# Attention with sink and window heads, then a gated feed-forward block: the order of all instructions from a list schedule in place of fixed interleaving

## Chip, cores, metric

One core of one Trainium2 chip. The metric is the device time of a run in microseconds (us), lower is better.

## What is computed

Four sequences of 768 positions, eight heads of 64. Heads 0, 2 and 6 attend to all earlier positions; the other five only to the first 4 positions and to the last 64. The attention output, 3072 x 512, goes through a gated block with weights 512 x 1536, 512 x 1536 and 1536 x 512.

```python
scores = scale * np.matmul(q, k.transpose(0, 1, 3, 2))
stream_keep = causal & (is_sink | in_win)
mask = np.where(retr[0, :, 0, 0, None, None], full_mask, stream_mask)
...
a = np.exp(scores)
a = a / (np.sum(a, axis=-1, keepdims=True) + 1e-09)
attn_out = np.matmul(a, v)
...
x = np.ascontiguousarray(attn_out.transpose(0, 2, 1, 3)).reshape(B * S, H * D)
g = x @ w_gate
silu = g * (1.0 / (1.0 + np.exp(-g)))
return silu * (x @ w_val) @ w_out
```

## The kernel before

Work is cut into 24 tiles of 128 positions; a pair is two tiles of one sequence (`QP`, 12 pairs, in the order sequence 0, 1, 0, 0, 1, 1, then 2 and 3). Tiles are gathered into seven groups of 2, 2, 4, 4, 4, 4, 4 (`SIZES`), over which the feed-forward block runs, so its matmuls have 256 columns in groups 0 and 1 and 512 in the others.

Of a pair: `load` brings queries, keys and values (512 KB each) into one of 11 `raw` buffers on the sync queue; `cast` makes half precision copies (`hq`; ScalarE for queries and keys, for pairs 0 and 1 VectorE and GpSimd for keys; GpSimd for values); `transposes` turns queries and keys by TensorE, eight 128 x 128 transposes at a time, into the one buffer `tr`, and VectorE evacuates them into `qkT` (L231). Calls go by row parity j, so that scores need both calls of a pair. GpSimd then copies the keys and values of sinks and of the previous block (`k2`, `v2`).

Of a tile: units of up to eight score matmuls into the one buffer `sc` (L292), the exponential by ScalarE into one of seven buffers `e` (L298, L302), masks multiplied in (`masks`; GpSimd, the large ones of the first four tiles VectorE), value matmuls for odd and for even heads into the one buffer `av` (L340), normalisation by VectorE (L343, L344), four transposes (`xtr`, L357) and their copy into the group's `xt` (L358).

Of a group: twelve times a gate quad (four matmuls, L446), tanh by ScalarE (L450), a val quad (L457) and two VectorE steps (L461, L464) that leave `h`. Gates and vals share three buffers of accumulator memory. Then per tile three quads of output matmuls (L480), one copy by ScalarE (L493) and a store on the sync queue. Weights are cast by ScalarE and GpSimd in turn (`wcast`), 12 gate and val pieces of 256 columns within group 0, six output pieces within group 1.

The order is written out. `items` is one list of attention steps, woven unit by unit (`weave`). In the loop over groups, after each gate, val or output quad a `beat` runs the masks left over and a fixed share of that list: group g's beats are spread evenly over the attention of group g + 1. Each engine takes its instructions in the order in which the program issues them, with waits on semaphores; `tc.manual_schedule()` leaves that order as it is.

Of the kernel before, what the change touches and what calls it, by code (L numbers as in the profile page):

```python
# [11 lines left out]
PSUM = bass.MemoryType.PSUM  # L12


@with_exitstack
def kernel(
# [13 lines left out]
    nc = tc.nc  # L30
# [15 lines left out]
    QP += [(b, n) for b in range(2, B) for n in range(NT // 2)]  # L46
    TILES = [(b, 2 * n + m) for b, n in QP for m in range(2)]
# [11 lines left out]

    ctx.enter_context(tc.manual_schedule())  # L60

    const = ctx.enter_context(tc.tile_pool(name="const", bufs=1))
    raw = ctx.enter_context(tc.tile_pool(name="raw", bufs=11))
    half = ctx.enter_context(tc.tile_pool(name="half", bufs=2))
    epool = ctx.enter_context(tc.tile_pool(name="epool", bufs=7))
    xpool = ctx.enter_context(tc.tile_pool(name="xpool", bufs=3))
    small = ctx.enter_context(tc.tile_pool(name="small", bufs=4))
    xtp = ctx.enter_context(tc.tile_pool(name="xtp", bufs=2))
    ffns = ctx.enter_context(tc.tile_pool(name="ffns", bufs=2))
    hpool = ctx.enter_context(tc.tile_pool(name="hpool", bufs=2 * NJ))  # L70
    opool = ctx.enter_context(tc.tile_pool(name="opool", bufs=2))
    ps_gv = ctx.enter_context(tc.tile_pool(name="ps_gv", bufs=3, space=PSUM))
    ps_o = ctx.enter_context(tc.tile_pool(name="ps_o", bufs=1, space=PSUM))
    ps_sc = ctx.enter_context(tc.tile_pool(name="ps_sc", bufs=1, space=PSUM))
    ps_av = ctx.enter_context(tc.tile_pool(name="ps_av", bufs=1, space=PSUM))
    ps_tr = ctx.enter_context(tc.tile_pool(name="ps_tr", bufs=1, space=PSUM))

# [8 lines left out]
    wod = moe_w_out.rearrange("(po p) n -> p po n", p=128)  # L86
    landed = {}

    def load(what):
        r = raw.tile([128, 1024], FP, name="raw", tag="raw")  # L90
        landed[what] = r
        kind, n = what
# [22 lines left out]
    def wcast(eng, kind, n):  # L115
# [6 lines left out]
        if eng is nc.scalar:  # L122
            eng.copy(out=dst, in_=src)
        else:
            eng.tensor_copy(out=dst, in_=src)
        freed()

    def whole(n):
        return [(kd, n) for kd in "qkx"]

    order = whole(0) + whole(1) + [(kd, n) for n in range(6) for kd in "gv"]
    order += whole(2) + whole(3) + [("o", n) for n in range(6)]
    order += [x for n in range(4, len(QP)) for x in whole(n)]
    at = [0]

    def freed(n=1):

        for _ in range(n):
            if at[0] < len(order):
                load(order[at[0]])  # L140
                at[0] += 1

    freed(11)


    ident = const.tile([128, 128], FH, name="ident")
    nc.gpsimd.memset(ident, 0.0)
    nc.gpsimd.affine_select(
        out=ident, in_=ident, compare_op=ALU.not_equal, fill=1.0,
        base=0, pattern=[[-1, 128]], channel_multiplier=1,  # L150
    )

    def keep(ap, base, qstep, kstep):
        nc.gpsimd.affine_select(
            out=ap, in_=ap, compare_op=ALU.is_ge, fill=0.0, base=base,
            pattern=[[qstep, 128]], channel_multiplier=kstep,
        )

    m0 = const.tile([128, 8, 128], FH, name="m0")
    m1 = const.tile([128, 2, 128], FH, name="m1")
    diag = const.tile([128, 128], FH, name="diag")
    band0 = const.tile([128, 128], FH, name="band0")
    nc.gpsimd.memset(diag, 1.0)
    keep(diag, 0, 1, -1)
    nc.gpsimd.memset(band0, 1.0)
    keep(band0, WIN - 1, -1, 1)
    nc.gpsimd.memset(band0[0:NSINK, :], 1.0)  # L170
    keep(band0, 0, 1, -1)
    nc.gpsimd.memset(m1, 1.0)
    keep(m1[:, 0, :], WIN - 1, -1, 1)
    keep(m1[:, 0, :], 0, 1, -1)
    keep(m1[:, 1, :], WIN - 1 - 128, -1, 1)
    nc.gpsimd.memset(m1[0:64, 1, :], 0.0)
    nc.gpsimd.memset(m1[0:NSINK, 1, :], 1.0)


    qkT = [const.tile([128, 2, 4, S], FH, name=f"qkT{n}") for n in range(2)]  # L180
    k2 = [const.tile([128, 4, 4, 128], FH, name=f"k2_{n}") for n in range(2)]
    vt = [const.tile([128, NT, 8, 66], FH, name=f"vt{n}") for n in range(2)]
    v2 = [const.tile([128, 4, 8, 66], FH, name=f"v2_{n}") for n in range(2)]
    for n in range(2):
        nc.gpsimd.memset(vt[n][:, :, :, 64:66], 1.0)
        nc.vector.memset(k2[n][:, :, :, 0:64], 0.0)
        nc.vector.memset(v2[n][0:64], 0.0)
    for n_, src in enumerate((band0, band0, band0, diag, band0, band0, diag, diag)):
        nc.vector.tensor_copy(out=m0[:, n_, :], in_=src)


    warm = ps_gv.tile([128, 512], FP, name="warm", tag="gv")
    for n in range(40):
        nc.tensor.matmul(warm[:, 0:128], ident, ident, start=True, stop=True)


    halves = {}

    def cast(n):

        b, pi = QP[n]
        hq = half.tile([128, 2, 2, 2, 256], FH, name="hq", tag="hq")
        for w, kd in enumerate("qk"):
            r = landed.pop((kd, n)).rearrange("p (h j d) -> p h j d", j=2, d=64)
            for j in range(2):
                o_ = hq[:, w, j].rearrange("p r (k d) -> p r k d", d=64)
                i_ = r[:, :, j].rearrange("p (k r) d -> p r k d", r=2)
                if n < 2 and w == 1:
                    (nc.gpsimd if j else nc.vector).tensor_copy(out=o_, in_=i_)
                else:  # L210
                    nc.scalar.copy(out=o_, in_=i_)  # L211
            freed()
        r = landed.pop(("x", n)).rearrange("p (m h d) -> p m h d", m=2, d=64)
        for m in range(2):
            nc.gpsimd.tensor_copy(out=vt[b % 2][:, 2 * pi + m, :, 0:64], in_=r[:, m])
        freed()
        halves[n] = hq

    def transposes(n, j):
        b, pi = QP[n]  # L220
        hq = halves[n]
        if n == 0 and j:
            tr = ps_gv.tile([128, 2, 4, 128], FH, name="tr", tag="gv")
        else:
            tr = ps_tr.tile([128, 2, 4, 128], FH, name="tr", tag="tr")
        for w in range(2):
            for p in range(4):
                nc.tensor.transpose(  # L228
                    tr[:, w, p, :], hq[:, w, j, p // 2, (p % 2) * 128:(p % 2 + 1) * 128], ident)
        T = qkT[b % 2]  # L230
        nc.vector.tensor_copy(  # L231
            out=T.rearrange("p w r (n j) -> p w r n j", j=2)[
                :, :, :, pi * 128:(pi + 1) * 128, j],
            in_=tr)
        if j == 0 or pi == 0:
            return
        K2, V, V2 = k2[b % 2], vt[b % 2], v2[b % 2]
        if pi == 1:
# [7 lines left out]
        for m in (2 * pi - 1, 2 * pi):
            nc.gpsimd.tensor_copy(
                out=K2[:, :, m - 1, 64:128], in_=T[:, 1, :, m * 128 + 64:(m + 1) * 128])
            nc.gpsimd.tensor_copy(out=V2[64:128, m - 1], in_=V[64:128, m])
# [19 lines left out]
    av_blocks = {}  # L269
    deferred = []  # L270

# [9 lines left out]

    def scores(t, u, unit):
        b, i = TILES[t]
        T = qkT[b % 2]
        sc = ps_sc.tile([128, 2, 4, 128], FP, name="sc", tag="sc")
        e = epool.tile([128, 2, 4, 128], FH, name="e", tag="e")
        for n in range(4):
            for s in range(2):
                if n < len(unit[s]):
                    h, _, _, kk, vv = unit[s][n]  # L290
                    p = SIDE[h][0]
                    nc.tensor.matmul(  # L292
                        sc[:, s, n, :], kk,
                        T[s * 64:s * 64 + 64, 0, p, i * 128:(i + 1) * 128])
                    av_blocks.setdefault((t, h), []).append((e[:, s, n, :], vv))
# [271 lines left out]
```

## Time and profile before

| | us |
|---|---|
| median of 3 runs (lowest, highest) | 300.4 (299.0, 302.36) |
| the profiled execution's own time | 300.72 |
| its span, first to last instruction | 299.0 |
| mean granted TensorE clock, share of full speed | 0.952 |
| busy: TensorE, VectorE, ScalarE, GpSimd | 264.3, 174.6, 147.8, 132.2 |

The span is what the profile's times refer to, from its first instruction; the execution's own time holds 1.7 us around it. PE is TensorE, PEld its weight loads, DVE VectorE, ACT ScalarE, POOL GpSimd, SP the sync engine, whose queue issues all loads and most stores. Matmuls are pipelined, so the busy time of one overlaps that of the next.

### The profile page before, as it was taken

The page shows a single profiled execution, that of the slowest core. Times are in us where ns is not written, and L with a number is a line of the kernel's source. Part 1 is how long each engine was busy: PE and PEld are TensorE (multiplying, and loading weights), DVE is VectorE, ACT ScalarE, POOL GpSimd, SP SyncE. Part 2 cuts the span into 40 slices and gives each one's busy share as a digit, 9 for nine tenths or more (in the row PEclk, how much of TensorE's full clock was granted, in tenths as well). Part 3 has the DMA queues.
Part 4 walks back from the last instruction along what each step waited for, and adds up shares of the span by engine and source line. Part 5 has one row for each costly group of instructions (what it writes and reads, how often), then busy time and mean ns, then how long its engine had stood idle before and what let it go on. Part 6 is the DMA issues. An engine that isn't in the chain of part 4 may idle for free.

```text
span 299.0 us, 5710 instructions
## 1 busy us (share of the span) xinstructions
PE 264.3 (88%) x2232; PEld 144.2 (48%) x2232; DVE 174.6 (58%) x331; ACT 147.8 (49%) x242; POOL 132.2 (44%) x195
## 2 busy tenths in 40 slices
PE   7356687869898997989999999999999998999995
PEld 7244465646564454544454545544454444444442
DVE  5546665844648476676675566784676455555500
ACT  3443838784493753825546653726444552232221
POOL 6172568893884641485536333476424230000000
PEclk9758879986999999999999999999999999999998
DMA  7999999999134170441310001001100001001012
GB/s 206 327 382 381 267 355 353 255 289 283 39 95 153 30 217 1 115 134 37 70 37 35 4 33 37 35 2 37 37 36 2 35 35 37 0 35 37 35 70 105
DMA packets 61514, 34.96 MB, mean 117 GB/s; under 512 B 26032, under 2 KB 57008, under 8 KB 61488
## 3 DMA queue, kind: packets, MB, share of 16 engines
q1 hardware_dynamic: 61344, 34.48, 38.0%
q8 instruction: 17, 0.28, 0.4%
q10 hardware_dynamic: 144, 0.13, 0.1%
q14 instruction: 9, 0.07, 0.1%
HBM read 28.31 MB, written 6.29 MB: 116 GB/s over the span
## 4 chain that ended last, share of the span: by engine, by line
PE 71%; DVE 14%; ACT 7%; issue 3%; DMA 2%; POOL 1%; SPq 0%; DVEq 0%; ACTq 0%
PE o_ps L480 20%; PE gate L446 18%; PE val L457 18%; PE sc L292 7%; DVE qkT L231 7%; PE av L340 5%; PE tr L228 3%; ACT hq L211 3%; PE xtr L357 2%; DVE sil L461 2%; ACT e L298 2%; DVE h L464 2%; DMA raw<-in_k_dram 2%; DVE xb L344 1%; ACT sig L450 1%
## 5 line engine op out<-in xcount | busy, mean ns | idle before, releaser
L461 DVE SCALAR_TENSOR_TENSOR sil<-sig,gate 128x512 f32<-128x512 f32 (+1 forms) x84 | 51.0, 607 | 54.5 <-ACT sig L450 54.2
L457 PE MATMUL val<-xt,wv_sb 128*128 128x512 f16 (+1 forms) x336 | 78.0, 356 | 2.0 <-DVE sil L461 2.0
L446 PE MATMUL gate<-xt,wg_sb 128*128 128x512 f16 (+1 forms) x336 | 78.6, 358 | 1.1 <-DVE xt L358 1.0
L450 ACT ACTIVATE sig<-gate 128x512 f32<-128x512 f32 (+1 forms) x84 | 45.3, 539 | 68.6 <-PE gate L446 68.6
L480 PE MATMUL o_ps<-wo_sb,h 128*128 128x512 f16 x288 | 73.1, 383 | 0.7 <-ACT o_sb L493 0.7
L298 ACT ACTIVATE e<-sc 128x1024 f16<-128x1024 f32 x48 | 49.1, 1023 | 39.5 <-PE sc L292 32.9
L464 DVE SCALAR_TENSOR_TENSOR h<-sil,val 128x512 f16<-128x512 f32 (+1 forms) x84 | 51.4, 612 | 12.9 <-PE val L457 4.6
L313 POOL TENSOR_TENSOR e<-e,m 128x1024 f16<-128x1024 f16 x18 | 38.2, 2123 | 28.9 <-ACT e L298 28.8
L457 PEld LDWEIGHTS <-wv_sb 128*128 128x128 f16 x336 | 30.4, 100 | 26.3 <-issue 2.4
L446 PEld LDWEIGHTS <-wg_sb 128*128 128x128 f16 x336 | 29.5, 101 | 24.8 <-issue 1.7
L292 PE MATMUL sc<-qkT 64*128 64x128 f16 x392 | 26.2, 225 | 16.1 <-DVE qkT L231 10.8
L480 PEld LDWEIGHTS <-h 128*128 128x128 f16 x288 | 25.9, 98 | 28.2 <-issue 1.7
L325 POOL TENSOR_TENSOR e<-e,diag 128x128 f16<-128x128 f16 x60 | 24.9, 426 | 28.7 <-ACT e L302 19.8
L231 DVE COPY qkT<-tr 128x1024 f16<-128x1024 f16 x24 | 31.0, 1296 | 8.1 <-PE tr L228 7.8
L292 PEld LDWEIGHTS <-qkT 64*128 64x128 f16 x392 | 14.7, 96 | 40.0 <-issue 24.3
L340 PEld LDWEIGHTS <-e 128*128 128x128 f16 x472 | 21.9, 102 | 12.7 <-DVE e L307 2.0
L340 PE MATMUL av<-vt,e 128*128 128x65 f16 x392 | 23.2, 200 | 3.3 <-DVE xb L344 1.8
L493 ACT COPY o_sb<-o_ps 128x512 f32<-128x512 f32 x23 | 13.4, 584 | 24.8 <-PE o_ps L480 24.8
L211 ACT CAST hq<-raw 128x512 f16<-128x512 f32 x44 | 24.0, 626 | 2.7 <-DMA raw<-in_q_dram 2.7
L322 POOL TENSOR_TENSOR e<-e,m 128x256 f16<-128x256 f16 x20 | 13.4, 668 | 24.3 <-ACT e L298 24.2
L344 DVE TENSOR_TENSOR xb<-av,rc 128x256 f16<-128x256 f32 x48 | 20.4, 425 | 1.7
L343 DVE RECIPROCAL rc<-av 128x4 f32<-128x4 f32 x48 | 8.6, 179 | 18.1 <-PE av L340 18.0
(50 smaller groups left out, 181.3 us busy)
## 6 DMA issues: line engine op xcount, KB each, us to landing
raw<-in_q_dram SPq DMA_DIRECT2D x12, 512.0 KB, 5.2
raw<-in_k_dram SPq DMA_DIRECT2D x12, 512.0 KB, 5.6
raw<-in_v_dram SPq DMA_DIRECT2D x24, 256.0 KB, 4.9
out_dram<-o_sb SPq DMA_DIRECT2D x23, 256.0 KB, 2.0
raw<-in_moe_w_gate_dram SPq DMA_DIRECT2D x6, 512.0 KB, 8.1
raw<-in_moe_w_val_dram SPq DMA_DIRECT2D x6, 512.0 KB, 8.4
raw<-in_moe_w_out_dram SPq DMA_DIRECT2D x6, 512.0 KB, 6.2
out_dram<-o_sb SPq DMA_DIRECT2D x1, 128.0 KB, 1.7
```

The lines of the kernel that those rows point to most:

```text
L211: nc.scalar.copy(out=o_, in_=i_)
L231: nc.vector.tensor_copy(out=T.rearrange("p w r (n j) -> p w r n j", j=2)[:, :, :, pi * 128:(pi + 1) * 128, j], in_=tr)
L292: nc.tensor.matmul(sc[:, s, n, :], kk, T[s * 64:s * 64 + 64, 0, p, i * 128:(i + 1) * 128])
L298: nc.scalar.activation(out=e[:, :, 0:na], in_=sc[:, :, 0:na], func=AF.Exp, scale=scale)
L313: (nc.vector if t < 4 else nc.gpsimd).tensor_tensor(out=ev, in0=ev, in1=m1.rearrange("p n q -> p (n q)").unsqueeze(1).to_broadcast([128, 4 ...
L340: nc.tensor.matmul(av[:, n, 0:65], ee, vv, start=(m == 0), stop=(m == len(bl) - 1))
L446: nc.tensor.matmul(ps, wg_sb[:, kk, j * 128:(j + 1) * 128], xt[:, kk, 0:w], start=(kk == 0), stop=(kk == 3))
L450: nc.scalar.activation(out=sig, in_=ps, func=AF.Tanh, scale=0.5)
L457: nc.tensor.matmul(pv, wv_sb[:, kk, j * 128:(j + 1) * 128], xt[:, kk, 0:w], start=(kk == 0), stop=(kk == 3))
L461: nc.vector.scalar_tensor_tensor(out=sil, in0=sig, scalar=1.0, op0=ALU.add, in1=ps, op1=ALU.mult)
L464: nc.vector.scalar_tensor_tensor(out=h, in0=sil, scalar=0.5, op0=ALU.mult, in1=pv, op1=ALU.mult)
L480: nc.tensor.matmul(o_ps, hs[g, j][:, tt * 128:(tt + 1) * 128], wo_sb[:, j, :], start=(j == 0), stop=(j == NJ - 1))
```

## The change

Every step is now a task with the engines that may run it (`ways`: engine, time that the engine is taken, time until the result is there), a place in the whole (`pos`), the tasks that it needs and the buffers that it takes. `Plan.order` builds the schedule: of all tasks that could start, it takes the engine with the earliest start, and on that engine, among tasks within 0.13 us, the one with the lowest `pos`. Loads are tasks of their own. The tasks are then issued in order of their start in this model. Lengths are constants in the code.

Beside the order: query and key transposes are cut by tensor (w) in place of by parity (j), so that one evacuation holds the queries and one the keys of a pair, written side by side and read with the two parities in turn; an evacuation may go to VectorE or ScalarE; each cast and each mask is a task by itself; weight casts may go to GpSimd or ScalarE, the first two pairs' casts of queries and keys to three engines; only the first two tiles' large masks are on VectorE; gates and vals are one function and one name (`gv`); gates may run ahead of vals. Matmuls, buffers and their numbers, loads and their order are the same.

```diff
+    INTO, BACK = 0.096, 0.120
...
+                for r in t.takes:
+                    n, held = self.rings[r]
+                    if len(held) >= n:
+                        us = self.users[held[-n], r]
+                        if any(u.start is None for u in us):
+                            ok = False
+                            break
+                        at0 = max([at0] + [u.end for u in us])
...
+                for w in t.ways:
+                    at = max(at0, free.get(w[0], 0.0))
+                    if w[0] == "PE" and last_kind.get("PE") is not None:
+                        a, b = last_kind["PE"] == "sc", t.kind == "sc"
+                        at += self.BACK if a and not b else self.INTO if b and not a else 0.0
+                    found.append((at, w, t))
...
+            at0, w0, _ = min(found, key=lambda x: x[0])
+
+            same = [x for x in found if x[1][0] == w0[0] and x[0] <= at0 + 0.13]
+            at, w, t = min(same, key=lambda x: (x[2].pos, x[0]))
+            t.start, t.end, t.way = at, at + w[2], w
+            free[w[0]] = at + w[1]
...
+        return sorted(done, key=lambda t: t.start)
...
+    def act(n):
+        return ("ACT", 0.083 + n * 0.000833, 0.225 + n * 0.000833)
...
+            T_w[kd, n] = P.add(
+                f"wc {kd}{n}", [pool(1.04), act(1024)], pos,
+                (lambda kd=kd, n=n: wcast(kd, n)), deps=[T_load[kd, n]])
...
+    A = 0.25
...
+        g, i = GROUP[t]
+        return g - 1 + i / SIZES[g] - A
...
+                ways = [act(512)] + ([dve(0.6), pool(0.85)] if n < 2 else [])
...
+            ev = T_ev[n, w] = P.add(f"ev{n}.{w}", [dve(1.3), act(1024)], pos - 0.05 + 0.02 * w,
+                                    (lambda n=n, w=w: evac(n, w)),
+                                    deps=[tr] + older + ([T_fill] if n == 0 else []))
...
+                ways = [dve(0.72)] if t < 2 and size == 1024 else [
+                    pool({1024: 2.12, 256: 0.667, 128: 0.425}[size])]
...
-    for g in range(NG):
-        start = pos[0]
-        stop = min(ends[FIRST[g + 2] - 1] + LA, len(items)) if g + 2 <= NG else len(items)
...
+    for task in P.order():
+        task.run()
```

ScalarE at the start, the old order. `hq` are casts of queries and keys, `e` exponentials of scores, with one buffer number for each; raw_105 holds pair 0's queries, raw_112 pair 1's, and the w casts are weights.

```order
L211 CAST hq_213<-raw_105 128x512 x2
L298 ACTIVATE e_247<-sc_246 128x1024
L298 ACTIVATE e_259<-sc_258 128x1024
L298 ACTIVATE e_280<-sc_279 128x1024
L211 CAST hq_309<-raw_112 128x512 x2
L123 CAST wg_sb_102<-raw_119 128x4x256
```

The same place in the new order; raw_192 and raw_194 hold pair 0's queries and keys, raw_228 pair 1's keys, `tr` are transposed queries or keys.

```order
L172 CAST hq_196<-raw_192 128x512 x2
L172 CAST hq_196<-raw_194 128x512
L172 COPY qkT0_117<-tr_202 128x4x256
L435 ACTIVATE e_241<-sc_232 128x1024
L172 CAST hq_230<-raw_228 128x512
L435 ACTIVATE e_270<-sc_249 128x1024
L435 ACTIVATE e_289<-sc_280 128x1024
L172 COPY qkT1_118<-tr_296 128x4x256
L172 CAST wg_sb_105<-raw_278 128x4x256
```

Here half a cast of pair 1's keys moved between the exponentials of tiles 0 and 1, and two evacuations came to ScalarE.

ScalarE from the first exponential of tile 4 on, the old order. sig is the tanh of a gate, hq_707 holds pair 3's casts.

```order
L298 ACTIVATE e_640<-sc_639 128x1024
L123 CAST wv_sb_103<-raw_354 128x4x256
L450 ACTIVATE sig_683<-gate_678 128x256
L298 ACTIVATE e_686<-sc_685 128x1024
L211 CAST hq_707<-raw_430 128x512 x2
L211 CAST hq_707<-raw_433 128x512 x2
L450 ACTIVATE sig_726<-gate_721 128x256
L302 ACTIVATE e_729<-sc_728 128x128
L302 ACTIVATE e_729<-sc_728 128x256
L450 ACTIVATE sig_757<-gate_752 128x256
L298 ACTIVATE e_782<-sc_781 128x1024
```

The same in the new order; hq_743 holds pair 3's casts.

```order
L435 ACTIVATE e_722<-sc_704 128x1024
L172 CAST hq_743<-raw_659 128x512
L642 ACTIVATE sig_757<-gv_738 128x256
L435 ACTIVATE e_764<-sc_747 128x1024
L172 CAST hq_743<-raw_691 128x512
L172 CAST hq_743<-raw_659 128x512
L439 ACTIVATE e_796<-sc_783 128x128
L439 ACTIVATE e_796<-sc_783 128x256
L172 CAST wo_sb_107<-raw_773 128x1024
L172 CAST hq_743<-raw_691 128x512
L172 CAST wo_sb_107<-raw_794 128x1024
L435 ACTIVATE e_867<-sc_824 128x1024
```

The four casts that stood in one piece stand apart, and tile 5's first exponential follows after one tanh in place of three.

The sync queue where the first store stands, the old order; one line is a load or a store, two of values make a pair's.

```order
L96 DMA raw<-in_q_dram 128x8x128
L96 DMA raw<-in_k_dram 128x8x128
L104 DMA raw<-in_v_dram 128x8x64 x2
L96 DMA raw<-in_q_dram 128x8x128
L96 DMA raw<-in_k_dram 128x8x128
L494 DMA out_dram<-o_sb 128x512
L104 DMA raw<-in_v_dram 128x8x64 x2
```

The new order around its first store, whose following load is that of pair 5's keys.

```order
L269 DMA raw<-in_q_dram 128x8x128
L269 DMA raw<-in_k_dram 128x8x128
L277 DMA raw<-in_v_dram 128x8x64 x2
L269 DMA raw<-in_q_dram 128x8x128
L681 DMA out_dram<-o_sb 128x512
L269 DMA raw<-in_k_dram 128x8x128
L277 DMA raw<-in_v_dram 128x8x64 x2
```

The first store moved from behind pair 8's keys to ahead of pair 5's.

## Rows read from the trace of the kernel before

**Rows 1.** The page: span, busy us, share and instructions.

```profile
span 299.0 us, 5710 instructions
...
PE 264.3 (88%) x2232; PEld 144.2 (48%) x2232; DVE 174.6 (58%) x331; ACT 147.8 (49%) x242; POOL 132.2 (44%) x195
```

**Rows 2.** Busy time by stage, with granted clock, DMA share and GB/s at the end.

```profile
core 0: us, PE busy (x) PEld busy (x) DVE busy (x) ACT busy (x) POOL busy (x), PEclk, DMA share, GB/s
0.00:20.20 20.20, 10.61 (x112) 8.85 (x113) 11.49 (x28) 8.50 (x10) 11.38 (x32) 0.76 0.99 296
20.20:42.90 22.70, 16.05 (x138) 11.46 (x139) 14.34 (x28) 10.69 (x18) 9.53 (x14) 0.76 1.07 334
42.90:88.10 45.20, 38.22 (x458) 26.42 (x458) 25.90 (x64) 31.36 (x56) 34.43 (x48) 0.92 0.78 225
88.10:252.90 164.80, 157.69 (x1339) 78.89 (x1336) 105.91 (x187) 85.59 (x139) 76.81 (x103) 1.00 0.18 54
```

**Rows 3.** The same view of two short stretches.

```profile
12.00:24.00 12.00, 7.25 (x61) 5.31 (x61) 6.11 (x16) 5.63 (x8) 6.69 (x10) 0.50 1.08 372
...
66.00:72.00 6.00, 6.00 (x54) 3.74 (x53) 2.45 (x8) 1.79 (x3) 2.50 (x3) 0.50 1.01 268
```

**Rows 4.** Timeline, TensorE: first gate, first scores of tile 4, group 2's first gate.

```profile
20.21 1.01 PE L446 MATMUL gate<-xt,wg_sb 128*128 128x256 f16 x4 [0.52 <-DVE xt L358]
...
42.85 0.23 PE L292 MATMUL sc<-qkT 64*128 64x128 f16 x2 [0.95 <-DVE qkT L231]
...
88.14 1.04 PE L446 MATMUL gate<-xt,wg_sb 128*128 128x512 f16 x4
```

**Rows 5.** Timeline, TensorE, three places without waits: start us, us, what, count.

```profile
54.77 0.60 PE L457 MATMUL val<-xt,wv_sb 128*128 128x256 f16 x4
55.21 0.19 PE L340 MATMUL av<-vt,e 128*128 128x65 f16 x1
...
93.81 0.61 PE L228 MATMUL tr<-ident,hq 128*128 128x128 f16 x8
94.26 1.03 PE L446 MATMUL gate<-xt,wg_sb 128*128 128x512 f16 x4
...
124.01 1.02 PE L480 MATMUL o_ps<-wo_sb,h 128*128 128x512 f16 x4
124.97 0.40 PE L292 MATMUL sc<-qkT 64*128 64x128 f16 x8
125.30 1.04 PE L446 MATMUL gate<-xt,wg_sb 128*128 128x512 f16 x4
126.17 0.29 PE L340 MATMUL av<-vt,e 128*128 128x65 f16 x4
126.30 1.02 PE L457 MATMUL val<-xt,wv_sb 128*128 128x512 f16 x4
```

**Rows 6.** The chain that ended last, its final long piece.

```profile
284.77 10.53 PE o_ps L480 x48
```

**Rows 7.** Timeline, ScalarE, 44 to 49 us.

```profile
44.20 1.04 ACT L123 CAST wv_sb<-raw 128x1024 f16<-128x1024 f32 x1
45.14 0.39 ACT L450 ACTIVATE sig<-gate 128x256 f32<-128x256 f32 x1
45.41 1.02 ACT L298 ACTIVATE e<-sc 128x1024 f16<-128x1024 f32 x1
46.32 2.18 ACT L211 CAST hq<-raw 128x512 f16<-128x512 f32 x4
48.39 0.40 ACT L450 ACTIVATE sig<-gate 128x256 f32<-128x256 f32 x1
```

**Rows 8.** Timeline, VectorE: the evacuation ahead of tile 4's scores.

```profile
41.49 1.29 DVE L231 COPY qkT<-tr 128x1024 f16<-128x1024 f16 x1 [0.34 <-PE tr L228]
```

**Rows 9.** Timeline, GpSimd: pair 2's first values, and a large mask.

```profile
34.97 0.61 POOL L215 CAST vt<-raw 128x512 f16<-128x512 f32 x1 [0.88 <-DMA raw<-in_v_dram]
...
51.36 2.12 POOL L313 TENSOR_TENSOR e<-e,m 128x1024 f16<-128x1024 f16 x1 [0.91 <-ACT e L298]
```

**Rows 10.** Timeline, TensorE at 65.7 us: idle time in brackets, and what ended it.

```profile
65.71 0.37 PE L292 MATMUL sc<-qkT 64*128 64x128 f16 x2 [1.89 <-ACT e L302]
```

More of the change, by code (lines that the diff above doesn't have):

```diff
@@ L87, with warm, load @@
+    def warm():
+        ps = buf("gv", [128, 512], FP, "warm")
+        for n in range(40):
+            nc.tensor.matmul(ps[:, 0:128], ident, ident, start=True, stop=True)
+    T_masks = P.add("masks", [("POOL", 6.6, 6.6)], -9.0, make_masks)
+    T_fill = P.add("fill", [("DVE", 6.9, 6.9)], -9.0, fill, deps=())
+    T_warm = P.add("warm", [("PE", 6.8, 6.8)], -9.0, warm, takes=["gv"])
+    P.uses(T_warm, "gv", T_warm)
     landed = {}
[L89 to L92, printed above, removed]
+    def load(kind, n):
+        r = buf("raw", [128, 1024], FP, "raw")
+        landed[kind, n] = r
@@ L113, in load, with whole, wcast @@
                 in_=(wgd if kind == "g" else wvd)[:, :, n * 256:(n + 1) * 256])
-    def wcast(eng, kind, n):
+    def whole(n):
+        return [(kd, n) for kd in "qkx"]
+    order = whole(0) + whole(1) + [(kd, n) for n in range(6) for kd in "gv"]
+    order += whole(2) + whole(3) + [("o", n) for n in range(6)]
+    order += [x for n in range(4, NP) for x in whole(n)]
+    T_load = {}
+    before = P.add("dma", [("DMA", 4.7, 4.7)], -9.0, lambda: None)
+    for at, (kd, n) in enumerate(order):
+        d = {"q": 1.45, "k": 1.45, "x": 2.2}.get(kd, 1.36)
+        before = T_load[kd, n] = P.add(
+            f"load {kd}{n}", [("DMA", d, d + 0.6)], at * 1e-3 - 5,
+            (lambda kd=kd, n=n: load(kd, n)), after=before, takes=["raw"])
+    T_w = {}
+    def wcast(kind, n):
         r = landed.pop((kind, n))
@@ L121, in wcast @@
             src = r.rearrange("p (a n) -> p a n", a=4)
[L122 to L199, printed above, removed]
-        b, pi = QP[n]
[L202 to L217, printed above, removed]
@@ L219, in transposes @@
-    def transposes(n, j):
-        b, pi = QP[n]
[L221 to L226, printed above, removed]
+        copy(T_w[kind, n], dst, src)
+    for n in range(6):
+        for kd in "gvo":
+            pos = 0.9 + n / 10 if kd == "o" else n / 6 - 0.3
+            T_w[kd, n] = P.add(
+                f"wc {kd}{n}", [pool(1.04), act(1024)], pos,
+                (lambda kd=kd, n=n: wcast(kd, n)), deps=[T_load[kd, n]])
+            P.uses(T_load[kd, n], "raw", T_w[kd, n])
@@ new lines, with place, cast @@
+    A = 0.25
+    def place(t):
+        g, i = GROUP[t]
+        return g - 1 + i / SIZES[g] - A
+    hqs = {}
+    def cast(n, kd, j):
+        b, pi = QP[n]
+        if n not in hqs:
+            hqs[n] = buf("hq", [128, 2, 2, 2, 256], FH, "hq")
+        r = landed[kd, n].rearrange("p (h j d) -> p h j d", j=2, d=64)
+        copy(T_c[n, kd, j],
+             hqs[n][:, "qk".index(kd), j].rearrange(
+                 "p r (k d) -> p r k d", d=64),
+             r[:, :, j].rearrange("p (k r) d -> p r k d", r=2))
@@ L227, in transposes, with castv @@
+    def castv(n, m):
+        b, pi = QP[n]
+        r = landed["x", n].rearrange("p (m h d) -> p m h d", m=2, d=64)
+        copy(T_c[n, "x", m], vt[b % 2][:, 2 * pi + m, :, 0:64], r[:, m])
+    trs = {}
+    def transposes(n, w):
+        tr = buf("tr", [128, 2, 4, 128], FH, "tr")
+        for j in range(2):
             for p in range(4):
                 nc.tensor.transpose(
-                    tr[:, w, p, :], hq[:, w, j, p // 2, (p % 2) * 128:(p % 2 + 1) * 128], ident)
-        T = qkT[b % 2]
@@ L246, in transposes, with evac @@
[L246 to L249, printed above, removed]
+                    tr[:, j, p, :],
+                    hqs[n][:, w, j, p // 2, (p % 2) * 128:(p % 2 + 1) * 128], ident)
+        trs[n, w] = tr
+    def evac(n, w):
+        b, pi = QP[n]
+        copy(T_ev[n, w],
+             qkT[b % 2][:, w, :, pi * 256:(pi + 1) * 256].rearrange("c p (n j) -> c p n j", j=2),
+             trs.pop((n, w)).rearrange("c j p n -> c p n j"))
@@ L344, in values, with xevac @@
         nc.vector.tensor_tensor(
-            out=xb[:, :, odd, :], in0=av[:, :, 0:64],
+            out=xbs[t][:, :, odd, :], in0=av[:, :, 0:64],
             in1=rc.to_broadcast([128, 4, 64]), op=ALU.mult)
-    xts = {}
     def xtranspose(t):
+        xb = xbs.pop(t)
+        tr = buf("tr", [128, 4, 128], FH, "xtr")
+        for p in range(4):
+            nc.tensor.transpose(tr[:, p, :], xb[:, p].rearrange("p a d -> p (a d)"), ident)
+        trs[t] = tr
+    def xevac(t):
         g, n = GROUP[t]
@@ L352, in xtranspose @@
         if g not in xts:
-            xts[g] = xtp.tile([128, 4, 512], FH, name="xt", tag="xt")
-        xb = xbs.pop(t)
-        tr = ps_tr.tile([128, 4, 128], FH, name="xtr", tag="tr")
-        for p in range(4):
-            nc.tensor.transpose(tr[:, p, :], xb[:, p].rearrange("p a d -> p (a d)"), ident)
-        nc.vector.tensor_copy(out=xts[g][:, :, n * 128:(n + 1) * 128], in_=tr)
-    items = []
-    ends = {}
-    def add(cost, f, *a):
-        items.append((cost, f, a))
-        if f is xtranspose:
-            ends[a[0]] = len(items)
@@ L530, with oevac @@
-    for n in range(SIZES[NG - 1] * 3):
-        outproj(NG - 1, n)
+    def oevac(g, tt):
+        o_sb = buf("osb", [128, DM], FP, "o_sb")
+        o_ps = o_open.pop((g, tt))
+        b, i = TILES[FIRST[g] + tt]
+        r0 = b * S + i * 128
+        if g == NG - 1 and tt == SIZES[g] - 1:
+            nc.scalar.copy(out=o_sb[:, 0:256], in_=o_ps[:, 0:256])
+            nc.sync.dma_start(out=out[r0:r0 + 128, 0:256], in_=o_sb[:, 0:256])
+            nc.vector.tensor_copy(out=o_sb[:, 256:512], in_=o_ps[:, 256:512])
+            nc.scalar.dma_start(out=out[r0:r0 + 128, 256:512], in_=o_sb[:, 256:512])
+        else:
+            nc.scalar.copy(out=o_sb, in_=o_ps)
+            nc.sync.dma_start(out=out[r0:r0 + 128, :], in_=o_sb)
```

533 lines of the change are left out of this document (346 added, 187 removed).

## The prediction

> **What bounds the kernel now.** I read the page's totals first [rows 1]: of a span of 299.0 us TensorE is busy 264.3 us, so its order decides before anything else. The run of this profile took 300.72 us, 1.7 beyond its span; the median shown is 300.4, so the sum below, made against this execution, stands 0.3 us above it.
>
> Busy time overstates the work, since matmuls overlap. So I took the distance from one start to the next in TensorE's timeline where nothing waits [rows 5]: four matmuls of 512 columns 0.87 us (0.216 each below), four of 256 columns 0.44, eight transposes 0.45, four value matmuls 0.13 (0.03 each). A block of eight score matmuls takes 0.33 to the next start, and the quad ahead of it 0.96 in place of 0.87: about 0.23 for its columns and 0.2 for going in and out. The order of instructions gives the counts, the same in both kernels: 768 matmuls of 512 columns (165.9), 192 of 256 (21.1), 288 transposes (16.1), 68 score blocks with 472 matmuls (27.8), 472 value matmuls (14.2). Sum 245.1 us. Some 54 us of the span is not work, and three marks say where it lies: the first gate, the first scores of tile 4, the first gate of group 2 [rows 4].
>
> From 88.1 us to TensorE's last matmul at 295.3 [rows 6] lie 207 us. Counted from the old order, 47.7 us of work stands ahead of that gate and 197.5 behind it: 9.5 us are lost there. The rest is lost before: TensorE is busy 10.6 of the first 20.2 us, 16.1 of the next 22.7 and 38.2 of the next 45.2 [rows 2], part of it at the lower granted clock [rows 3].
>
> **The change part by part.** No matmul is added or taken away. What moves is the order on every queue, the owner of some copies, and the cut of the query and key transposes (by tensor in place of by row parity).
>
> *Owners.* Ten of 24 evacuations of transposed tiles and three more weight casts go to ScalarE, which the order shows as COPY qkT and CAST w. An evacuation on ScalarE is not in this trace. The nearest rows are an exponential of the same width, read from the same memory, with 0.91 to the next start [rows 7], and the 1.29 that VectorE takes for an evacuation now [rows 8]. The new evacuation reads its two parities alternately; for that the far end is the slowest operation of 1,024 columns shown, 2.12 us on GpSimd [rows 9]. A gain is not excluded either, since VectorE now writes side by side what it wrote in every second place. I take 1.0 on ScalarE and 1.3 on VectorE, the rows of the same operation; at 2.12 the scores of some eight later pairs would each start 0.8 us later, 6 us in all, which the range holds. Over the kernel ScalarE gains 10 x 1.0 + 3 x 0.94 = 13 us and VectorE is relieved of as much. ScalarE was busy 85.6 of the 164.8 us of the long stage [rows 2], so this is hidden unless a copy stands in front of an exponential that is waited for (rival 3). Two big masks of 2.12 us go from VectorE to GpSimd, which gives up three casts for them.
>
> *To 42.9 us.* On ScalarE the cast of half of pair 1's keys now stands ahead of tile 1's first exponential, and waits for its load; on VectorE the other half's cast stands ahead of tile 0's mask. Both pairs are transposed, and tiles 2 and 3 partly scored, before the first gate, which I expect about 1 us later than 20.2. That costs nothing at the end, since group 0 is paced by its weights. The Trainium skill, "TensorE: Matmul & The Clock Gate", section "Architectural detail: the array is 16× 32×32, not 1× 128×128", calls ScalarE and VectorE strict first in, first out, which speaks against ready work behind a cast that waits. By it the exponential and the mask wait until that load lands; by a queue that let ready work pass, the first gate would stand where it stood, and the sum would be the same.
>
> What limits this stage is loads: 20.2 us at 296 GB/s and 22.7 at 334 [rows 2] make 13.6 MB, and everything up to pair 3 is 24 loads of 524 KB, 12.6 MB, there by about 40 us in either order. Pair 2's first values land at 34.9 [rows 9], its keys before them, at about 34. From there: two casts of 0.52 [rows 7], transposes 0.45, an evacuation of 1.0 to 1.3, near a second for the one transpose buffer, and three quads of 0.44 that the order puts ahead: tile 4's scores start at about 38.5, against 42.85. By then the new order has 17.3 us of work behind it, the old one 13.8.
>
> *From there to the first gate of group 2.* This is the stage that pays. Work of TensorE: 45.9 - 17.3 = 28.6 us. ScalarE, by distances of starts [rows 7]: 11 exponentials of 0.92 (10.1), 8 shorter ones of 2,816 columns together (2.9, by width), 16 casts of 0.52 (8.3), 12 tanh of 0.27 (3.2), 4 weight casts of 0.94 (3.8), two output copies (0.9, by width), one evacuation (1.0): 30.2 us. GpSimd was busy 34.4 us in this stage before [rows 2], for three score blocks more. So the earliest is 38.5 + 30.2 = 68.7; the latest, at the old pace of 45.2 us for the stage, 83.7. Before, four casts at a time stood ahead of exponentials, and TensorE once stood 1.89 us for the only score buffer [rows 7, 10]; the new order puts casts singly into gaps. With three engines at some 29 to 34 us, and a chain of score, exponential, mask and value between them, I do not take the lower end but 36.5 us: the gate stands at 75.
>
> TensorE's granted clock was 0.50, 1.2 GHz, from 66 to 72 us, as from 12 to 24 [rows 3], and just ahead of 66 TensorE stood idle [rows 10]. If the fall comes again, the six busy microseconds hold three of full work, and the gate stands at 78. The skill's same page, section "What's actually happening", says that the lower rate is the default and activity lifts it; by it a denser order keeps the full clock and the sum stays, by the row alone it may be 3 us more. I keep 75.
>
> *Behind it.* 245.2 - 45.9 = 199.3 us of work. Of the 9.5 us lost there before, much was spent waiting for evacuated tiles just ahead of scores. The new order puts gates, vals or output quads (0.87 each) between, so I take 5; bounds 2 and 9.5. The last 48 output matmuls are unchanged, and from their end to the span's lie 3.7 us [rows 6]. On the sync queue the first store now stands ahead of pair 5's keys, and waits for the first output tile; pair 5 serves tiles 10 and 11 of group 3, some 30 us later, which covers it.
>
> Sum: 75 + 199.3 + 5 + 3.7 + 1.7 = 284.7, **285 us**. Lower end 68.7 + 199.3 + 2 + 3.7 + 1.7 = 275; upper end 83.7 + 199.3 + 9.5 + 3.7 + 1.7 = 298.
>
> **Rivals.**
> 1. *Nothing comes of the order, since loads and the chain of attention pace the start.* For it: the DMA share is 1.07 up to 42.9 us, and four tiles need 14 exponentials one behind another. Against it: that share falls to 0.78 in the stage that pays [rows 2]. Then group 2 starts at 83.7 and 9.5 are lost behind: 298.
> 2. *The order does all that its lengths allow*: 68.7 and 2, 275 us. For it: the fixed order wastes most where the work is most mixed. Against it: three engines would have to be nearly full.
> 3. *Slower: exponentials come late in the long stage.* There is one score buffer. Block, exponential and release take 0.33 + 1.02 + 0.1 = 1.45 us, and the order puts one or two quads (0.87 to 1.73) between blocks. A copy or a tanh in front of the exponential then comes out on TensorE. 46 blocks stand behind group 2's first gate; at 0.40 us each they cost 18.4, and 285 becomes 303.4, from where on it is slower by 1%. At 0.45 it is 305. For it: more copies on ScalarE, and little reserve between blocks. Against it: ScalarE is about half busy in that stage, so most exponentials find it free.
>
> **How the numbers follow.** My case, 278 to 292: 0.66. Rival 2: 0.14. Rival 1: 0.13, of which a third lies beyond a gain of 1%. Rival 3: 0.07. A measurement of this kernel tells about 1% from no change. So faster 0.84, same 0.09, slower 0.07. The range from 275 to 298 leaves out rival 3 and the tips of the others.
>
> **What would show it.** Right: first scores of tile 4 near 38.5 us, first gate of group 2 near 75, no clock of 0.50 around 66 to 72 us, TensorE losing about 5 us behind that gate, evacuations near 1.0 us on ScalarE. Wrong: that gate after 82 us; waits of scores for exponentials above 10 us in sum; evacuations near 2 us.

## The result: 286.3 us, and the profile after

| | us |
|---|---|
| after, median of 4 runs | 286.29 (285.07 to 286.9) |
| before, measured beside it | 299.7 (298.3 to 302.36) |
| ratio, 95% interval | 0.954 (0.946 to 0.962) |
| the profiled execution of after | 285.07 |

The predicted time was 285, so the number held. Of the marks on the way to it, the first two did not. The page of after, its totals and its load queue, answers to [rows 1]:

```profile
span 283.4 us, 5690 instructions
...
PE 261.6 (92%) x2232; PEld 142.3 (50%) x2232; DVE 161.5 (57%) x319; ACT 160.3 (57%) x255; POOL 133.7 (47%) x194
...
q1 hardware_dynamic: 61344, 34.48, 45.0%
```

The marks on TensorE's timeline, as in [rows 4]: the first gate, tile 4's first scores, group 2's first gate.

```profile
23.23 1.01 PE L635 MATMUL gv<-xt,wg_sb 128*128 128x256 f16 x4
...
41.60 0.23 PE L421 MATMUL sc<-qkT 64*128 64x128 f16 x2
...
75.58 0.59 PE L635 MATMUL gv<-xt,wg_sb 128*128 128x512 f16 x2
```

Busy time between these marks (columns as in [rows 2]); the last stretch ends at the first gate of group 6:

```profile
0.00:23.23 23.23, 13.37 (x145) 11.19 (x146) 13.19 (x28) 12.02 (x14) 15.26 (x36) 0.70 1.05 269
23.23:41.60 18.37, 15.85 (x148) 11.36 (x146) 11.92 (x31) 13.95 (x24) 12.54 (x17) 0.91 1.07 302
41.60:75.58 33.98, 31.15 (x381) 21.29 (x381) 20.47 (x50) 30.22 (x55) 27.28 (x39) 0.95 1.09 281
75.58:238.06 162.48, 159.67 (x1375) 79.78 (x1372) 98.26 (x185) 92.46 (x145) 78.66 (x105) 1.00 0.26 69
```

| mark | before | predicted | after |
|---|---|---|---|
| first gate | 20.2 | about 21.2 | 23.2 |
| first scores of tile 4 | 42.9 | 38.5 | 41.6 |
| first gate of group 2 | 88.1 | 75 | 75.6 |
| lost behind it | 9.5 | 5 | 4.8 |

The last row is worked out as in the prediction: TensorE's last matmul ends at 279.66, 204.1 us behind the gate, for 199.3 us of work. The gain is there by group 2: 12.6 us of the 15.6 by which the span shrank. Two things were not expected. The start is late, and the loads are slower: the queue q1 took 45.0% of 283.4 us, 128 us, for the same 34.48 MB; before, it took 38.0% of 299.0 us, 114 us.

ScalarE, VectorE and GpSimd at the start show both. Pair 0's keys land 1.86 us behind its queries: their casts start, as the loads land, at 6.80 and 4.94. VectorE's cast of pair 1's keys takes 2.27 us.

```profile
4.94 1.14 ACT L172 CAST hq<-raw 128x512 f16<-128x512 f32 x2 [2.85 <-DMA raw<-in_q_dram]
6.80 0.62 ACT L172 CAST hq<-raw 128x512 f16<-128x512 f32 x1 [0.72 <-DMA raw<-in_k_dram]
...
12.82 2.27 DVE L174 CAST hq<-raw 128x512 f16<-128x512 f32 x1 [2.57 <-DMA raw<-in_k_dram]
...
12.30 1.94 POOL L371 COPY v<-vt 4x2112 f16<-4x2112 f16 x1
14.20 0.61 POOL L174 CAST vt<-raw 128x512 f16<-128x512 f32 x1
```

What TensorE waited for, summed over the span (us, times, longest):

```profile
PE av L463 <- POOL e L454: 2.7, 2, 2.1
PE sc L421 <- ACT e L435: 2.3, 3, 1.1
...
PE sc L421 <- DVE qkT L174: 1.3, 1, 1.3
```

So rival 3, late exponentials, cost 2.3 us. TensorE's granted clock no longer falls at 66 us [rows 3] but at 50, behind two microseconds in which TensorE was half idle:

```profile
48.00:50.00 2.00, 1.02 (x10) 0.64 (x10) 0.68 (x3) 2.00 (x3) 0.32 (x1) 1.00 1.00 370
50.00:53.50 3.50, 3.38 (x25) 1.69 (x23) 2.85 (x6) 3.29 (x6) 3.12 (x3) 0.56 1.03 381
```

Nearly all of that idle time, 0.96 us, is a wait of TensorE's transposes for a cast of pair 3's keys on ScalarE. The keys were there, for their other half had been cast at 44.70; but this cast stands behind one of output weights, for whose load ScalarE waited 1.46 us:

```profile
49.37 0.40 PE L355 MATMUL tr<-ident,hq 128*128 128x128 f16 x4 [0.96 <-ACT hq L172]
...
47.74 1.05 ACT L172 CAST wo_sb<-raw 128x1024 f16<-128x1024 f32 x1 [1.46 <-DMA raw<-in_moe_w_out_dram]
48.70 0.61 ACT L172 CAST hq<-raw 128x512 f16<-128x512 f32 x1
```

### The profile page after: what moved, and what is told of

It is laid out like the page before. It is cut to its first block, busy times and chain, and to the rows that moved or that the text cites. A ratio compares the mean times of both kernels' runs of the same rounds, so it can differ in the third digit from the quotient of the medians.

```text
span 283.4 us, 5690 instructions
## 1 busy us (share of the span) xinstructions
PE 261.6 (92%) x2232; PEld 142.3 (50%) x2232; DVE 161.5 (57%) x319; ACT 160.3 (57%) x255; POOL 133.7 (47%) x194
## 3 DMA queue, kind: packets, MB, share of 16 engines
q1 hardware_dynamic: 61344, 34.48, 45.0%
## 4 chain that ended last, share of the span: by engine, by line
PE 75%; DMA 13%; SPq 3%; ACT 2%; DVE 2%; issue 2%; POOL 1%; ACTq 0%; POOLq 0%
PE gv L635 39%; PE o_ps L665 18%; DMA raw<-in_k_dram 10%; PE sc L421 6%; PE av L463 5%; PE tr L355 3%; DMA raw<-in_v_dram 2%; PE xtr L480 2%; PE gv L665 2%; SPq L277 2%; SPq L269 1%; DMA raw<-in_moe_w_out_dram 1%; POOL e L454 1%; ACT e L435 1%; ACT hq L172 1%
## 5 line engine op out<-in xcount | busy, mean ns | idle before, releaser
L647 DVE SCALAR_TENSOR_TENSOR sil<-sig,gv 128x512 f32<-128x512 f32 (+1 forms) x84 | 51.1, 609 | 45.8 <-ACT sig L642 45.6
L635 PE MATMUL gv<-xt,wv_sb 128*128 128x512 f16 (+1 forms) x336 | 76.5, 353 | 0.7 <-DVE sil L647 0.7
L642 ACT ACTIVATE sig<-gv 128x512 f32<-128x512 f32 (+1 forms) x84 | 44.6, 538 | 55.9 <-PE gv L635 55.8
L635 PE MATMUL gv<-xt,wg_sb 128*128 128x512 f16 (+1 forms) x336 | 75.2, 352 | 0.0
L454 POOL TENSOR_TENSOR e<-e,m 128x1024 f16<-128x1024 f16 (+1 forms) x42 | 59.7, 1433 | 24.0 <-ACT e L435 23.6
L665 PE MATMUL o_ps<-wo_sb,h 128*128 128x512 f16 x264 | 67.6, 380 | 0.1
L654 DVE SCALAR_TENSOR_TENSOR h<-sil,gv 128x512 f16<-128x512 f32 (+1 forms) x84 | 51.2, 611 | 15.7 <-PE gv L635 12.1
L463 PEld LDWEIGHTS <-e 128*128 128x128 f16 x472 | 19.4, 99 | 13.9 <-POOL e L454 4.7
L174 DVE COPY qkT<-tr 128x1024 f16<-128x1024 f16 x14 | 17.1, 1222 | 7.2 <-PE tr L355 7.1
L378 POOL COPY k<-qkT 128x256 f16<-128x256 f16 x16 | 6.4, 397 | 30.7 <-DVE qkT L174 21.4
```

What stands on the lines that cost most here:

```text
L174: ENG[task.way[0]].tensor_copy(out=dst, in_=src)
L454: eng.tensor_tensor(out=ev, in0=ev, in1=mm, op=ALU.mult)
L463: nc.tensor.matmul(av[:, n, 0:65], ee, vv, start=(m == 0), stop=(m == len(bl) - 1))
L635: nc.tensor.matmul(ps, wsb[:, kk, j * 128:(j + 1) * 128], xt[:, kk, 0:w], start=(kk == 0), stop=(kk == 3))
L642: nc.scalar.activation(out=sg[g, j], in_=gs[g, j], func=AF.Tanh, scale=0.5)
L647: nc.vector.scalar_tensor_tensor(out=sl[g, j], in0=sg.pop((g, j)), scalar=1.0, op0=ALU.add, in1=gs.pop((g, j)), op1=ALU.mult)
```

## Experiments

My theory was that the gain is in the order; the rivals were the owners and the loads. Ratios are to the kernel before on the same chip, with 95% intervals.

**The two kernels once more.**

> The kernel before, unchanged, to see its landing times and queue share once more beside the kernel after on the same chip. If the slower loads of the kernel after come of the change, this run shows pair 2's keys landing near 34 us and the load queue at about 114 us again. If they come of the run or the chip, it shows landings and a share near those of the kernel after (38 us, 128 us) when that one does. Time 299 to 301 in either case.

> The kernel after, unchanged. If its late marks at the start (first gate 23.2 us, first scores of tile 4 41.6 us) belong to its order, they come again within 0.5 us, with VectorE's cast of pair 1's keys again above 2 us. If they belong to that run's loads, the first scores of tile 4 come near 38.5 us, where the prediction had them, and the end moves by at most as much. Time 285 to 287.

Before took 300.86 us in one run; after 286.67, ratio 0.954 (0.949 to 0.959). The marks of after came again (23.37, 41.91, 75.71), as did the cast of 2.27 us. The queue share of after was 45.1%, that of before 38.4%:

```profile
q1 hardware_dynamic: 61344, 34.48, 38.4%
```

That is 115 us of 299.2 against 129 of 285.2, on one chip. So the slower loads belong to the program. They are slower from the second one on, before the order can matter.

**Owners and order apart.** In the old kernel:

```diff
-        for w in range(2):
+        for jj in range(2):
...
+        if w and n >= 2:
+            nc.scalar.copy(out=dst, in_=src)
...
-                (nc.vector if t < 4 else nc.gpsimd).tensor_tensor(
+                (nc.vector if t < 2 else nc.gpsimd).tensor_tensor(
...
-                wcast(nc.gpsimd if j % 2 else nc.scalar, "o", j)
+                wcast(nc.scalar, "o", j)
```

> The old fixed interleaving with the new owners and the new cut of transposes alone: keys of pairs 2 to 11 evacuated by ScalarE, two large masks moved to GpSimd, all six output weight casts on ScalarE. Theory, the gain is in the order: 297 to 301, group 2's first gate at 86 to 90 us. Rival, the gain is in relieving VectorE: 292 or less, group 2's gate near 80 us, and the waits of TensorE for evacuations behind that gate gone.

296.32 us, ratio 0.989 (0.982 to 0.995), group 2's gate at 90.2. That is 0.7 us below the theory's range and far from the rival's 292: a gain of 1%, which came behind that gate, 203.6 us to TensorE's last matmul against 207.2. The waits that the rival named did shrink there. Scores waited 4.5 us for evacuations on VectorE in the kernel before (first line), and 1.2 us for those on ScalarE here (second line):

```profile
PE sc L292 <- DVE qkT L231: 4.5, 6, 1.5
```

```profile
PE sc L295 <- ACT qkT L235: 1.2, 5, 0.3
```

In the new kernel, the owners back (the casts of the first two pairs too):

```diff
-[dve(1.3), act(1024)]
+[dve(1.3)]
...
-                ways = [dve(0.72)] if t < 2 and size == 1024 else [
+                ways = [dve(0.72)] if t < 4 and size == 1024 else [
...
-[pool(1.04), act(1024)]
+[act(1024) if (n + (kd == "v")) % 2 == 0 else pool(1.04)]
```

> The new list schedule with the old owners: all 24 evacuations on VectorE, four large masks on VectorE, weight and key casts where they were; the new cut of transposes stays. Theory, the gain is in the order: 285 to 289, group 2's first gate at 74 to 78 us. Rival, the gain is in the owners: 294 or more.

287.2 us, ratio 0.958 (0.951 to 0.965), group 2's gate at 76.8. Not told apart from after: the order carries the gain, and under it the owners bring nothing that can be measured. Two things stay open. Both kernels have the slower loads of the next part, and what the owners bring without them was not run. And the new cut of the transposes is in own and in oldown, so no run has it alone; in own, it and the owners together bring 1%.

**Why the loads are slower.** The section on the change calls the buffers the same. Their numbers are, but not their places: the change also allocates the pool `small` ahead of the raw buffers. Its four `rc` buffers take 128 bytes of each partition, and in the built programs all raw buffers began at 110720 + 4096 n in place of 110592 + 4096 n.

```diff
-    small = ctx.enter_context(tc.tile_pool(name="small", bufs=4))
-    for r in ("raw", "hq", "e", "xb", "xt", "sig", "sil", "h", "osb"):
+    for r in ("raw", "hq", "e", "xb"):
         pools[r] = ctx.enter_context(tc.tile_pool(name="p_" + r, bufs=RINGS[r]))
+    small = ctx.enter_context(tc.tile_pool(name="small", bufs=4))
+    for r in ("xt", "sig", "sil", "h", "osb"):
+        pools[r] = ctx.enter_context(tc.tile_pool(name="p_" + r, bufs=RINGS[r]))
```

> The kernel after, with the small pool for rc allocated behind xb again, as before the change. Its 128 bytes had moved all 11 raw buffers from byte 110592 to 110720 of a partition. Nothing else differs, the order is the same. Theory, the slower loads come of that shift: query and key loads come 1.49 us apart again in place of 1.86, the load queue's share is about 114 us in place of 128, first scores of tile 4 at 38.5 to 39.5 us in place of 41.9, group 2's first gate at 73 to 74, time 283 to 285. Rival, they come of the denser order of loads: loads unchanged, time 286 to 287.

278.89 us, ratio 0.934 (0.926 to 0.942). Loads at the old pace (1.49 us apart, 41.5% of 276.5, 115 us), and 4 us more gained than the theory's range held:

```profile
span 276.5 us, 5690 instructions
...
q1 hardware_dynamic: 61344, 34.48, 41.5%
```

```profile
4.80 1.14 ACT L174 CAST hq<-raw 128x512 f16<-128x512 f32 x2 [2.72 <-DMA raw<-in_q_dram]
6.29 0.62 ACT L174 CAST hq<-raw 128x512 f16<-128x512 f32 x1 [0.34 <-DMA raw<-in_k_dram]
```

Its stages, cut at the same marks, and ten microseconds of the third:

```profile
0.00:22.02 22.02, 13.17 (x144) 10.63 (x145) 13.37 (x28) 12.29 (x14) 15.47 (x36) 0.69 0.99 303
22.02:39.41 17.39, 15.25 (x146) 11.42 (x145) 11.73 (x31) 13.38 (x23) 11.97 (x16) 0.91 1.07 329
39.41:70.08 30.67, 29.93 (x382) 20.73 (x382) 20.30 (x50) 30.00 (x55) 27.58 (x40) 1.00 1.02 296
...
50.00:60.00 10.00, 10.00 (x132) 6.69 (x129) 5.92 (x17) 9.96 (x20) 8.49 (x14) 1.00 0.94 257
```

Tile 4's scores come 2.2 us earlier than in after. The stage behind them takes 30.7 us in place of 34.0: TensorE has no idle stretch at 48 us and keeps its clock (1.00 against 0.95). The same work, from the transposes ahead of that stretch to the next value matmuls, takes 3.8 us (46.06 to 49.82) in place of 6.2 (48.02 to 54.20). ScalarE is now busy 30.0 of 30.7 us and TensorE 29.9; which of the two sets the length no run separates. In all the last matmul ends 6.9 us earlier (272.81).

In the kernel before, the line of `small` moved ahead of that of `raw`:

> The kernel before, with the small pool allocated ahead of the raw buffers, as the change has it, and nothing else. Theory: loads 1.86 us apart for queries and keys, share 128 us; the first stages are late by some 2 to 4 us and the time is 302 to 304. Rival: loads as in the kernel before, 300 to 301.

303.62 us, ratio 1.016 (1.009 to 1.023): slower with the shift alone. The queue's 42.3% of 303.1 are 128 us, and pair 0's keys land 1.85 us behind its queries. So it isn't the denser order of loads, the rival under align. In the old order the shift costs 4.3 us (303.62 against 299.34).

In the kernel after, eight `rc` buffers:

```diff
-    small = ctx.enter_context(tc.tile_pool(name="small", bufs=4))
+    small = ctx.enter_context(tc.tile_pool(name="small", bufs=8))
```

> The kernel after with eight rc buffers in place of four in the small pool, so that the raw buffers begin 256 bytes behind their old place, at byte 110848 of a partition, in place of 128 behind it; the order is the same. If only a start that is no multiple of 256 is slow: query and key loads 1.49 us apart, queue share as in align, time 278 to 281. If a row of 512 bytes must begin at a multiple of 512: 1.86 us apart, as in the kernel after, time 285 to 287.

```profile
4.79 1.14 ACT L172 CAST hq<-raw 128x512 f16<-128x512 f32 x2 [2.71 <-DMA raw<-in_q_dram]
6.30 0.62 ACT L172 CAST hq<-raw 128x512 f16<-128x512 f32 x1 [0.37 <-DMA raw<-in_k_dram]
```

Loads 1.51 us apart, 279.54 us, ratio 0.936 (0.928 to 0.945): 256 bytes off costs nothing that can be measured. 128 bytes off costs 7.4 us by the medians of after and align, which were measured apart; by their ratios, each to the kernel before measured beside it, it is 2.0% of that kernel's time, 5.9 us. Other starts were not tried. The shift moves the buffers of `hq`, `e` and `xb` too; ScalarE's casts into `hq` take 1.14 and 0.62 us either way.

The Trainium skill, "DMA: Bandwidth & Descriptors", section "How a descriptor splits into AXI transactions", says that a descriptor is cut into transactions of 256 bytes, and that one which starts off a 256-byte boundary fetches from the boundary below. It says this of reading; here the shifted side is written. Worked out from it, an estimate, a row of 512 bytes at an offset of 128 takes 20 beats of 32 bytes in place of 16, a factor of 1.25; the trace has 1.86 / 1.49 = 1.25. The shortest rows do not fit: for the 256 bytes of the values the same estimate gives 12 beats in place of 8, a factor of 1.5, and pair 0's first values land 1.2 us behind the keys in after and 0.9 in align, a factor of 1.3. So these beats are a candidate for the cause, not shown to be it.

**The slow cast.** In align, moved in the finished order:

```diff
-    for task in P.order():
+    todo = P.order()
+    late = [t for t in todo if t.name == "sinks0"]
+    todo = [t for t in todo if t not in late]
+    at = 1 + next(i for i, t in enumerate(todo) if t.name == "wc v5")
+    for task in todo[:at] + late + todo[at:]:
         task.run()
```

> The kernel align, with GpSimd's copies of the sinks of sequence 0 (0.24 and 1.94 us, first needed by tile 4) moved behind its last weight cast of group 0. Theory, VectorE's cast of pair 1's keys took 2.27 us because it ran beside that copy: it takes 0.43 us, the first gate stands about 2 us earlier (near 21 us), the end moves by under 1 us since loads pace tile 4. Rival, the cast is slow by itself: 2.27 us again. If the start is paced by the first gate and not by loads, the end comes 2 us earlier.

```profile
11.60 0.43 DVE L176 CAST hq<-raw 128x512 f16<-128x512 f32 x1 [1.90 <-DMA raw<-in_k_dram]
```

In align itself it stood beside that copy:

```profile
11.44 2.04 DVE L176 CAST hq<-raw 128x512 f16<-128x512 f32 x1 [1.60 <-DMA raw<-in_k_dram]
...
11.26 1.94 POOL L373 COPY v<-vt 4x2112 f16<-4x2112 f16 x1
```

The cast takes 0.43 us in place of 2.04, the first gate stands at 20.5 in place of 22.0, and the time is 279.59, ratio 0.935 (0.929 to 0.941): no gain at the end. So the copy on four partitions had held VectorE up. In align the cast ended 0.28 us behind the end of that copy; in after, where it took 2.27 us, 0.28 us behind the end of the GpSimd cast that followed the copy without a gap. The Trainium skill, "SBUF — State Buffer", section "Who interferes with whom", has this rule: a cast on VectorE in a two-port mode and a GpSimd instruction share a port pair that one of them holds for its whole instruction. The trace agrees, 0.43 us against 2.04 and 2.27; which mode the cast ran in no view shows.

**Loads in another order**, in align:

```diff
-    order = whole(0) + whole(1) + [(kd, n) for n in range(6) for kd in "gv"]
-    order += whole(2) + whole(3) + [("o", n) for n in range(6)]
+    w_ = [(kd, n) for n in range(6) for kd in "gv"]
+    order = whole(0) + whole(1) + w_[:6] + whole(2) + w_[6:8] + whole(3) + w_[8:]
+    order += [("o", n) for n in range(6)]
```

> The kernel align, with the loads of pairs 2 and 3 moved ahead in the load order: behind the first six and the first eight of the twelve gate and val weight pieces in place of behind all twelve; the list schedule follows from it. Theory, loads of pairs 2 and 3 pace the stage from tile 4's scores to group 2's first gate: tile 4's scores near 33 us, group 2's gate at 68 to 71 us, time 279 to 282. Rival, ScalarE and the chain of attention pace it, or group 0's late weights take back what is won: group 2's gate at 73 or later, time 284 or more.

278.79 us, ratio 0.934 (0.927 to 0.941). Tile 4's scores came at 33.9, as the theory had them, and the gate at 69.0; the time is just below its range, and the rival's 284 did not come. But both ranges were set before align's time was known, and against align they decide nothing: tile 4's scores came 5.5 us earlier, group 2's gate 1.0, and the end did not move. So with loads at the old pace, pairs 2 and 3 no longer set the end.

**What in the schedule carries the gain**, each in align:

```diff
-        return ("ACT", 0.083 + n * 0.000833, 0.225 + n * 0.000833)
+        return ("ACT", 0.5 * (0.083 + n * 0.000833), 0.5 * (0.225 + n * 0.000833))
...
-            same = [x for x in found if x[1][0] == w0[0] and x[0] <= at0 + 0.13]
+            same = [x for x in found if x[1][0] == w0[0] and x[0] <= at0]
```

The first edit (with the same for VectorE and GpSimd) is align_half, the second align_tol0.

> The kernel align with a schedule made with wrong lengths: all operations of ScalarE, VectorE and GpSimd planned at half their time, TensorE's and the loads as they were. The program is scheduled anew and does the same work. Theory, the gain rests on calibrated lengths, since a plan with too short exponentials and masks puts too little work of TensorE behind each score block: 284 to 295, with TensorE waiting for exponentials and masks 8 us or more in sum. Rival, priorities and buffer rules carry the gain and lengths matter little: 278 to 282.

322.08 us, ratio 1.081 (1.073 to 1.090), far above the theory's range. TensorE waits 15.6 us for masks and 12.4 for exponentials:

```profile
PE av L465 <- POOL e L456: 15.6, 18, 2.0
PE sc L423 <- ACT e L437: 12.4, 27, 1.3
```

> The kernel align with a schedule that always takes the earliest start on an engine, and the place in the whole only among equal starts: the window of 0.13 us is set to 0, lengths stay right. Theory, the gain needs priorities beside lengths, since strictly earliest first lets work of later tiles pass work that is needed now: 288 or more, group 2's first gate after 76 us. Rival, lengths alone carry it: 278 to 282.

317.8 us, ratio 1.067 (1.058 to 1.075), group 2's gate at 95.3, as the theory had it, and scores wait 17.1 us for exponentials:

```profile
PE sc L423 <- ACT e L437: 17.1, 17, 5.0
```

A list schedule is not better by itself. With the lengths of three engines at half, or without the window in which priority decides, the same scheduler is 19 to 23 us slower than the interleaving by hand.

**The clock at the start**, in align:

```diff
+    fill_ps = buf("o", [128, DM], FP, "o_ps")
+    pe_free = 7.6
     for task in P.order():
+        if task.way[0] == "PE" and 8 < task.start < 30:
+            for _ in range(min(16, int(0.5 * (task.start - pe_free) / 0.056))):
+                nc.tensor.matmul(fill_ps[:, 0:128], ident, ident, start=True, stop=True)
...
```

> The kernel align with 102 idle matmuls of 128 columns put into TensorE's queue in the gaps of its schedule up to the first gates, from the warming to 30 us. They write into the output accumulator, which is not yet in use; the order of the rest is the same. TensorE's granted clock was 0.50 from about 8 to 26 us in align. Theory, the half clock at the start costs 1 to 3 us, since work of the first two groups runs at half rate there: with the gaps filled the clock stays above 0.9, the first gate stands at 20 to 21.3 us in place of 22.0, group 2's first gate at 68 to 69.5 in place of 70.1, time 276 to 278. Rival, loads and the chain on the other engines pace the start: the clock rises and the marks stay within 0.5 us, time 278 to 280; if the fillers stand in front of work that is waited for, 280 or more.

From 20 to 24 us the granted clock is 1.00 (first line), where align had 0.50 (second line):

```profile
20.00:24.00 4.00, 3.71 (x59) 2.91 (x58) 1.25 (x5) 3.58 (x6) 3.69 (x3) 1.00 1.09 385
```

```profile
20.00:24.00 4.00, 3.26 (x26) 2.11 (x24) 1.03 (x3) 2.92 (x5) 3.95 (x4) 0.50 1.09 385
```

The first gate stands at 22.1, as in align, tile 4's scores at 38.8, 0.6 us earlier, and group 2's gate at 72.2, 2.1 us later. The time is 277.84, ratio 0.926 (0.920 to 0.932). So the time lies in the theory's range and the marks do not, and the profiled run (279.8 us) is the longest of the six. The time is not told apart from align, whose interval overlaps. In the profiled run the half clock at the start did not set the marks; a gain of about 1% stays open.

## Why the prediction was right, and where not

The number was right by luck in one place: two terms were wrong by about the same, in opposite directions. Tile 4's scores came 3.1 us later than 38.5, and the stage behind them took 2.5 us less than 36.5. The terms behind group 2's gate were right.

- *Loads ("there by about 40 us in either order")*: wrong. They paced the start as said, but pair 3's last values landed at 46.1 us, against 42.1 before and 41.3 in align. I read the load order and took the loads as unchanged; the line of the diff that puts `small` ahead of the raw buffers I did not price. It costs 5.9 to 7.4 us. At tile 4's scores it is 2.2 of the 3.1 us; the other 0.9 stays in align, though pair 2's keys land at 33.8 there, near the 34 that the prediction took. What holds the scores there stays open.
- *From tile 4's scores to group 2 ("I do not take the lower end but 36.5")*: too long. With loads at the old pace it is 30.7 us, half a microsecond from the lower end of 30.2, which was ScalarE's work laid end to end; ScalarE and TensorE were both nearly full. In after it is 34.0, because of late loads and the clock: ScalarE's wait for a late weight load, TensorE's idle time behind it and the granted clock of 0.56 that followed. The plan in the code counts 1.45 us for a load of queries or keys, near the pace without the shift; whether a plan with the slower lengths would have lost less was not run.
- *First gate, about 1 us later*: 3 us. Align and align_sink split it: 1.2 us are the loads, 1.5 the cast held up by GpSimd, and 0.3 are left for the order. That it costs nothing at the end was right.
- *Owners*: evacuations on ScalarE 1.01 us (1.0 taken), on VectorE 1.22 (1.3), ScalarE 12.5 us busier (13). That they hide, with the slower loads in place, is shown by oldown. With the old order they and the new cut bring 1%.
- *Behind the gate, 5 us*: 4.8. The waits for evacuations are gone as said; 2.1 us of what stays is one wait for masks that stood on GpSimd behind casts waiting for a late load.
- *The clock*: the fall at 66 us went and another came at 50; align has neither.
- *The tail*: 3.7 us again.
- *Rivals*: rival 2 (275) is near what the order does without the shift (278.9); what spoke against it, three engines nearly full, is what align shows for ScalarE and TensorE, with GpSimd at 27.6 of 30.7 us. Rival 1's 83.7 for the gate was refuted, though loads did pace the start. Rival 3 did not happen, but its mechanism is real: in align_half scores wait 12.4 us for exponentials.

## What to carry to other kernels

A schedule planned from lengths is worth as much as its lengths and priorities: right, it took 7% here (align), with the lengths of three engines at half it lost 8%. Where a change touches the order in which pools are allocated, look at where the buffers of the loads begin, and keep them on multiples of 256 bytes: 128 bytes in front of them cost about a third of what the order gained (5.9 to 7.4 of some 20 us). And when a total comes out as predicted, check its marks all the same.

## What the runs showed of the hardware that I had not expected

Loads into buffers that start 128 bytes past a multiple of 256 are slower: rows of 512 bytes 1.86 us per 512 KB against 1.49, and the whole queue 128 us against 115. And a GpSimd copy on only four partitions (1.94 us) holds up a cast on VectorE until it has ended (align, 2.04 us in place of 0.43), or until the GpSimd cast next in line has ended too (after, 2.27 us).
